# Hash-bucketed attention and a maxout FFN: heads 4 to 7 of the first batch as one set turned by VectorE, with new first copies, burst distance, halved sums and end buffers

## The chip, the core and the metric

The kernel runs on one core of a Trainium2 chip. The metric is the device time of one execution in microseconds (us); the time before is the median of three runs. A profile of one execution shows when each engine was busy: PE is TensorE's matmuls and PEld its weight loads, DVE is VectorE, ACT is ScalarE, POOL is GpSimd, and SP is SyncE, which here only issues transfers.

## The reference

Four batches of eight heads, 768 positions, head dimension 64. Each query and each key gets a bucket number from the signs of six projections; a query attends only to the keys of its own bucket. The attention output is the input of a feed-forward net with a maximum over three branches.

```python
q_bits = (np.einsum('bhsd,dk->bhsk', q, proj) > 0).astype(np.int64)
k_bits = (np.einsum('bhsd,dk->bhsk', k, proj) > 0).astype(np.int64)
q_bucket = np.sum(q_bits * powers, axis=-1)
k_bucket = np.sum(k_bits * powers, axis=-1)
mask = q_bucket[:, :, :, None] == k_bucket[:, :, None, :]
scores = np.where(mask, scale * np.matmul(q, k.transpose(0, 1, 3, 2)), -1000000000.0)
attn = softmax(scores)
x = np.matmul(attn, v) with the heads of one position side by side: (3072, 512)
h = np.maximum(np.maximum(x @ w1, x @ w2), x @ w3)
out = h @ w_out
```

Inputs and output are float32. The kernel rounds to bf16 and fp16 on the way; the hash projections are made in float32.

## The kernel before, in words

**Scores.** For each head the kernel builds a tile S of 72 rows: 64 rows of the transposed and scaled q (or k) and up to 8 rows of hash bits as plus or minus 0.5. One matmul of a k block with q columns gives the score and the number of equal bits at once, and the exponential (L301, ScalarE) is shifted so that keys of another bucket vanish. The work is cut into 192 units (`units`), each of 768 score columns: `scores(u)` makes two or three matmuls (L293) into a PSUM tile of which there are two, and one exponential into one of 24 weight tiles AT. Batch 0 is cut in three chunks of 256 queries (chunks 0 to 2, two units a head, 48 units in all), the others in two chunks of 384 (chunks 3 to 8, three units a head). Units 0 to 23 are heads 0 to 3 of batch 0, and units 24 to 47 heads 4 to 7; unit 24 is the first of head 4.

**Bursts.** When four heads of a chunk are done, a burst follows: `sums` adds the weights up by matmuls with ones (L345), VectorE makes reciprocals of them (L352 to L356), `values` multiplies the weights with v (L367, two sides), and VectorE writes the scaled result to xT (L374). From chunk 3 on, VectorE first adds the three AT tiles of a head into one of 768 columns (`add`, L324), and the sums run over its two halves. A burst of chunks 3 to 8 is placed two units after the last unit of its heads. In batch 0 the first three bursts stand at units 20 to 30, one piece to a unit.

**Feed-forward.** `ffn_groups(c)` gives groups of four matmuls (L396), whose maximum VectorE keeps (L405), and then the output rows (L433, copied by L437 and stored on SP's queue). A list `ffn` is worked off at about one group a unit; the rest runs behind the last unit. The output rows are copied to tiles `osb` of which there are two; the very last row block is made in two halves, copied by ScalarE (L418) and VectorE (L420).

**Where S comes from.** There are two ways.

- *Pairs* (heads 0 to 7 of batch 0, pairs 0 to 3): TensorE turns a head (`pair_turn`, L120, three transposes), VectorE or ScalarE copies it to T32 (`pair_keep`), GpSimd scales it into S (`pair_place`, L134), TensorE projects it (`pair_hash`, L147, or `head_hash`, L167), and VectorE writes the bits (L150 or L172); for pairs 2 and 3 the bits go to S by eight transfers on SP's queue (L156).
- *Sets of four heads* (all later ones): VectorE turns 32x32 blocks (`turn`, L198, four a side), GpSimd narrows to bf16 (`narrow`, L203, two a side), four transfers on SP's queue place the rows in S (`place`, L208), TensorE projects (`quad_hash`, L217), VectorE makes bits (L220), and four transfers on SP's queue send them to S (L228): k first half, k second half, q first half, q second half, each for all four heads.

**Order.** The order of instructions on each engine is the order in which the program writes them (a manual schedule). The loop over units writes the scores of unit u+1 and then what `when(u, ...)` has put there: loads, turns, copies; then feed-forward groups, and then the bursts. An engine, and each queue of transfers, works strictly in that order: a transfer written behind a waiting one on SP's queue waits with it, and so does an operation of GpSimd behind the loads that GpSimd issues. `load_v`, `load_weights` and most of `load_quad` are issued by GpSimd.

**The start.** Pair 0 is loaded in single heads. VectorE fills two columns behind each block of the AT tiles (L463). Meanwhile twelve matmuls on a tile called `warm` keep TensorE busy (L472). Then the first head is turned, copied, hashed and placed by hand-written steps, and unit 0 follows.

Of the kernel before, what the change touches and what calls it, by code (L numbers as in the profile page):

```python
# [17 lines left out]
def kernel(  # L18
# [15 lines left out]
    P = 128  # L34
# [19 lines left out]
    LAG = 1  # L54
# [25 lines left out]
    warm = at_tiles[-1][:, 0:HALF]  # L80
# [61 lines left out]
    def pair_hash(pi):  # L142
        i, bp = bank()
        for side in (1, 0):
            for hd in range(2):
                g = 2 * side + hd
                nc.tensor.matmul(bp[Q * g : Q * (g + 1), 0:HALF], pj2[:, :],  # L147
                                 t32[pi][:, side, hd * HALF : (hd + 1) * HALF], start=True, stop=True)
        bits = b_pool.tile([P, HALF], BF16, tag="bits", name="bits")
        nc.vector.tensor_scalar(out=bits[:], in0=bp[:, 0:HALF], scalar1=0.0, scalar2=0.5,  # L150
                                op0=AluOp.is_gt, op1=AluOp.subtract)
        give(i)
        for hd in range(2):
            for side in (1, 0):
                g = 2 * side + hd
                nc.sync.dma_start(s_of[pi][D : D + NBITS, g, :].rearrange("b (c n) -> b c n", c=2),  # L156
                                  bits[Q * g : Q * g + 2 * NBITS, :])


# [157 lines left out]
    def add(c, h, n):  # L317
# [67 lines left out]
    def ffn_groups(c):  # L385
# [23 lines left out]

        def last(part, tb):  # L410
# [5 lines left out]
            osb = o_pool.tile([P, DM], FP32, tag="osb", name="osb")  # L416
# [7 lines left out]
        for tb in range(w // P):  # L424
            def go2(part, tb=tb):
# [9 lines left out]
                if part == 1:  # L435
                    osb = o_pool.tile([P, DM], FP32, tag="osb", name="osb")
                    nc.scalar.copy(osb[:], ps[:, 0:DM])  # L437
                    give(k_)
                    nc.sync.dma_start(rows[block_of(b, q0 // P + tb)], osb[:])
# [8 lines left out]
    with tc.manual_schedule():  # L448
# [8 lines left out]
        load_pair(2, nc.sync)  # L457
        load_pair(3, nc.sync)
        nc.gpsimd.memset(pj[:], 0.0)
# [4 lines left out]
        for hd in range(2):  # L464
            for u in range(2):
                nc.vector.tensor_copy(pj2[hd * D + u * Q : hd * D + (u + 1) * Q, hd : hd + 2 * NBITS - 1 : 2], pst[:, u, :])
# [11 lines left out]
        i1, mk1 = bank()  # L478
        bq = sc_ps.tile([P, 2, 512], FP32, tag="sc", name="bp")[:, 0, :]
# [3 lines left out]
        pair_keep(0, 0, 0, mq)  # L483
        head_hash(bk, 0, 1, 0)
        head_hash(bq, 0, 0, 0)
        pair_turn(0, 1, 1, mk1)
        first_place(1, 0, 0, mk)
        head_bits(bk, 0, 1, 0, 0)
        first_place(0, 0, 0, mq)
        head_bits(bq, 0, 0, 0, 0)  # L490
        give(iq)
        first_place(1, 0, 1, mk)
        head_bits(bk, 0, 1, 0, 1)
        give(ik)
        give(ib)
        pair_place(0, 0, 1, 0, 1)
        i2, mq1 = bank()
        pair_turn(0, 0, 1, mq1)
        pair_keep(0, 1, 1, mk1, nc.scalar)
# [126 lines left out]
```

## Time and profile before

| | |
|---|---|
| median of 3 runs | 277.81 us (276.68 to 278.61) |
| the profiled execution | 277.43 us, its span 275.6 us |
| mean granted TensorE clock | 0.992 |
| exponentials (L301) | 192, 152.7 us, 816 ns each |
| feed-forward matmuls (L396) | 648, 115.0 us |
| score matmuls (L293) | 432, 93.5 us |
| value matmuls (L367) | 864, 37.7 us (four run at a time) |
| sums, chunks 3 to 8 (L345, 384 columns) | 96, 8.2 us |
| VectorE turns (L198) | 48, 26.6 us, 561 ns each |
| adds of weights (L324) | 96, 53.9 us |
| DMA moved | 30.97 MB, 114 GB/s over the span |

The span is the time from the first to the last instruction of the core; the execution's own time is a little longer. Busy times of different engines overlap. In lists of groups, each line names the line of the kernel, the engine, the operation, what is written and read, and how often; "idle before" is the engine's own idle time ahead of the instructions, with the one that ended it. In the timeline, a line is a run of equal instructions: start, length, engine, what, count, and in brackets the idle time before. SPq and POOLq lines are the issue of a transfer, not the transfer.

### The profile page before, as it was taken

What the parts mean: (1) busy time and instruction counts of PE and PEld (TensorE: products, weight loads), DVE (VectorE), ACT (ScalarE), POOL (GpSimd) and SP (SyncE); (2) the same over time, 40 slices, a digit from 0 to 9 for tenths busy, and PEclk for the clock granted to TensorE, in tenths of its full rate; (3) what the DMA queues carried; (4) which work ended last, traced back from release to release, by engine and by line L of the source; (5) the groups of instructions that cost most, each with busy time, mean ns of one, the idle gap of its engine ahead of it and who ended that gap; (6) DMA issues with size and microseconds to landing.
All of it is one profiled execution on the core that took longest, in us unless ns stands there. A gap on an engine that the chain in (4) does not pass through costs nothing.

```text
span 275.6 us, 6502 instructions
## 1 busy us (share of the span) xinstructions
PE 263.2 (95%) x2538; PEld 158.6 (58%) x2538; DVE 196.0 (71%) x486; ACT 179.1 (65%) x260; POOL 68.0 (25%) x108
## 2 busy tenths in 40 slices
PE   7899999999999979999999999999999999999992
PEld 3555667865666645565555555555555555555651
DVE  3686787965886996996684898797657674865440
ACT  2888876648767860966859586683868769571321
POOL 3699550374100350285000062140000000000000
PEclk9999999999999997999999999999999999999999
DMA  7979999979921157169912036622020003001203
GB/s 226 287 158 165 221 245 227 209 125 231 246 49 40 38 145 115 53 183 251 168 40 76 2 81 148 160 57 63 33 95 0 1 4 114 2 0 40 76 2 114
DMA packets 20398, 30.97 MB, mean 112 GB/s; under 512 B 2608, under 2 KB 14736, under 8 KB 20368
## 3 DMA queue, kind: packets, MB, share of 16 engines
q0 software_dynamic: 8384, 14.16, 26.9%
q1 hardware_dynamic: 11552, 15.88, 19.2%
q10 hardware_dynamic: 432, 0.52, 0.6%
q8 instruction: 20, 0.33, 0.5%
q14 instruction: 10, 0.08, 0.1%
HBM read 25.17 MB, written 6.29 MB: 114 GB/s over the span
## 4 chain that ended last, share of the span: by engine, by line
PE 86%; DVE 7%; ACT 2%; issue 2%; DMA 1%; DVEq 0%; ACTq 0%
PE ms L396 31%; PE sc L293 22%; PE ms L367 11%; PE ms L433 11%; PE ms L345 4%; PE ms L217 3%; ACT AT L301 2%; DVE ad L324 2%; PE ms L472 1%; DVE ht L405 1%; PE ms L120 1%; PE ms L147 1%; PE ms L167 1%; DVE S L172 1%; DMA out_dram<-osb 1%
## 5 line engine op out<-in xcount | busy, mean ns | idle before, releaser
L301 ACT ACTIVATE AT<-sc 128x768 f16<-128x768 f32 x192 | 152.7, 816 | 66.4 <-PE sc L293 58.6
L396 PE MATMUL ms<-xT,w_sb 128*128 128x384 f16 (+1 forms) x648 | 115.0, 308 | 0.7 <-DVE ht L405 0.7
L293 PE MATMUL sc<-S 72*128 72x384 bf16 (+1 forms) x432 | 93.5, 308 | 2.6 <-ACT AT L301 1.9
L396 PEld LDWEIGHTS <-w_sb 128*128 128x128 f16 x648 | 62.6, 97 | 36.9 <-issue 1.5
L405 DVE TENSOR_TENSOR ht<-ht,ms 128x384 f16<-128x384 f16 (+1 forms) x108 | 54.3, 503 | 37.3 <-PE ms L396 35.4
L293 PEld LDWEIGHTS <-S 72*128 72x128 bf16 (+1 forms) x432 | 39.5, 98 | 34.0 <-issue 14.1
L203 POOL TENSOR_SCALAR T<-T 128x768 bf16<-128x768 f32 x24 | 21.8, 907 | 101.2 <-DVE T L198 80.4
L367 PE MATMUL ms<-AT,vo 128*32 128x385 f16 (+3 forms) x864 | 37.7, 318 | 0.0
L433 PE MATMUL ms<-wout_sb,ht 128*128 128x512 f16 x138 | 35.4, 378 | 0.0
L367 PEld LDWEIGHTS <-vo 128*32 128x32 f16 x864 | 25.1, 99 | 9.3 <-issue 1.3
L324 DVE TENSOR_TENSOR ad<-AT,AT 128x768 f16<-128x768 f16 x48 | 27.4, 572 | 2.8 <-ACT AT L301 2.8
L324 DVE TENSOR_TENSOR ad<-ad,AT 128x768 f16<-128x768 f16 x48 | 26.5, 551 | 2.5 <-ACT AT L301 1.2
L198 DVE STREAM_TRANSPOSE T<-nat 128x384 f32<-128x384 f32 x48 | 26.6, 561 | 0.0
L401 ACT CAST ht<-ms 128x384 f16<-128x384 f32 x36 | 17.2, 477 | 8.8 <-PE ms L396 8.7
L374 DVE SCALAR_TENSOR_TENSOR xT<-ms,sv,rb 128x384 f16<-128x384 f32 (+1 forms) x36 | 19.9, 568 | 2.6 <-PE ms L367 1.3
L433 PEld LDWEIGHTS <-ht 128*128 128x128 f16 x138 | 13.3, 97 | 13.3 <-DVE ht L405 0.8
L437 ACT COPY osb<-ms 128x512 f32<-128x512 f32 x23 | 13.4, 582 | 10.7 <-PE ms L433 9.6
L352 DVE STREAM_TRANSPOSE ys<-ms 128x384 f32<-128x384 f32 (+1 forms) x18 | 9.7, 536 | 8.0 <-PE ms L345 7.8
L134 POOL TENSOR_SCALAR S<-T 64x384 bf16<-64x384 f32 (+1 forms) x21 | 13.2, 627 | 3.8 <-ACT T L127 1.6
L192 POOL DMA_DIRECT2D nat<-in_k_dram x20 | 11.1, 563 | 3.6 <-DMA nat<-in_k_dram 2.2
L192 POOL DMA_DIRECT2D nat<-in_q_dram x20 | 11.1, 566 | 2.7 <-DMA vo<-in_v_dram 1.8
L345 PEld LDWEIGHTS <-ones 128*32 128x32 f16 x240 | 5.4, 95 | 8.8 <-issue 8.7
(48 smaller groups left out, 121.9 us busy)
## 6 DMA issues: line engine op xcount, KB each, us to landing
out_dram<-osb SPq DMA_DIRECT2D x23, 256.0 KB
S<-T SPq DMA_DIRECT2D x48, 96.0 KB
nat<-in_k_dram POOLq DMA_DIRECT2D x20, 192.0 KB, 7.5
nat<-in_q_dram POOLq DMA_DIRECT2D x20, 192.0 KB, 7.1
vo<-in_v_dram POOLq DMA_DIRECT2D x8, 384.0 KB, 8.2
w_sb<-in_moe_w_dram POOLq DMA_DIRECT2D x3, 768.0 KB, 7.2
nat<-in_k_dram SPq DMA_DIRECT2D x6, 192.0 KB
nat<-in_k_dram SPq DMA_DIRECT2D x3, 384.0 KB
```

The costliest lines, as they stand in the source:

```text
L192: eng.dma_start(dst, src)
L198: nc.vector.transpose(t32[name][:, u, half * HALF : (half + 1) * HALF], i_)
L203: nc.gpsimd.tensor_scalar(out=t16[name][:, u, :], in0=t32[name][:, u, :], scalar1=RS, scalar2=1.0, op0=AluOp.mult, op1=AluOp.mult)
L293: nc.tensor.matmul(views[j], s_of[kn][0 : D + bits, kx, m * P : (m + 1) * P], s_of[qn][0 : D + bits, qx, q0 : q0 + w], start=True, stop=True)
L301: nc.scalar.activation(t[:, :, 0:w], whole, ActFn.Exp, bias=-SCALE * 0.25 * bits, scale=SCALE)
L324: nc.vector.tensor_tensor(out=sum_of[c, h][:], in0=t[0], in1=t[n], op=AluOp.add)
L367: nc.tensor.matmul(av[Q * x : Q * (x + 1), 0:n], v_at[2 * b + i][:, x, cb * D + side : (cb + 1) * D : 2], weights_of(c, 4 * i + x, m)[:, 0 ...
L374: nc.vector.scalar_tensor_tensor(out=xt_of(c)[:, 2 * i + side, 0:w], in0=av[:, 0:w], scalar=sv_of[b, i, side][:], in1=rb[0][:, 0:w], op0=A ...
L396: nc.tensor.matmul(ps[:, 0:w], w_sb[wi][:, jc, fb * P : (fb + 1) * P], xt[:, jc, 0:w], start=(jc == 0), stop=(jc == NJC - 1))
L401: nc.scalar.copy(hts[fb][:, 0:w], ps[:, 0:w])
L405: nc.vector.tensor_tensor(out=hts[fb][:, 0:w], in0=hts[fb][:, 0:w], in1=ps[:, 0:w], op=AluOp.max)
L433: nc.tensor.matmul(ps[:, 0:DM], hts[fb][:, tb * P : (tb + 1) * P], wout_sb[:, fb, :], start=(fb == 0), stop=(fb == NFB - 1))
```

## The change

- Heads 4 to 7 of batch 0 are no longer pairs 2 and 3 but set 1: two times four loads on SP's queue, VectorE's turns at units 6 to 9 (k) and 10, 12, 13, 14 (q), GpSimd's narrows at 7, 9, 12 and 14, the places at 9 and 14, the hash behind unit 16 and its bits at 17. The turned blocks of a set of batch 0 keep the key order that `block_of` expects.
- The start: `warm` uses 256 columns that no fill touches, in 14 matmuls; the first k copy is VectorE's and the first q copy ScalarE's; the first k rows are placed by GpSimd; the hash is made in single matmuls for each half, alternately for k and q; the copies of head 1 go from ScalarE to VectorE. Unit 0's scores stand before the transposes of head 1.
- On GpSimd, the clearing and filling of `pj` moves behind the start, `load_v(0)` to unit 2 and the k load of set 2 from unit 1 to unit 4. The operand pj2 is filled half by VectorE and half by GpSimd.
- Bursts of chunks 3 to 8 stand four units behind, not two; the hashes of sets 4 to 7 stand two units later.
- From chunk 4 on, VectorE adds the two halves of a head's summed weights once more, and the sums take one block instead of two.
- The output rows of the last chunk are copied into three parts of one large tile, not into the two `osb` tiles.

```diff
-    LAG = 1
+    LAG = (1, 4)
...
-    warm = at_tiles[-1][:, 0:HALF]
+    warm = at_tiles[-1][:, THIRD + 2 : 2 * THIRD + 2]
...
-    def head_hash(bp, pi, side, hd):
-        for par in range(2):
+    def head_hash(bp, pi, side, hd, pars=(0, 1)):
+        for par in pars:
...
-        i_ = nat[name].rearrange("p (cc m u d) -> p u m cc d", cc=CC, u=2, d=Q)[:, u, half * MH : (half + 1) * MH]
+        ms = slice(half, NM, 2) if name[1] == 1 else slice(half * MH, (half + 1) * MH)
+        i_ = nat[name].rearrange("p (cc m u d) -> p u m cc d", cc=CC, u=2, d=Q)[:, u, ms]
...
+        if n == 2 and c > 3:
+            t = sum_of[c, h]
+            nc.vector.tensor_tensor(out=t[:, 0, :], in0=t[:, 0, :], in1=t[:, 1, :], op=AluOp.add)
...
-            return [t[:, j, 0:w] for j in range(2)]
+            return [t[:, j, 0:w] for j in range(1 if c > 3 else 2)]
...
+        def out_rows(tb):
+            if c < NCH - 1:
+                return o_pool.tile([P, DM], FP32, tag="osb", name="osb")
+            if "end" not in nat:
+                nat["end"] = nat_pool.tile([P, 4 * NM * D], FP32, tag="nat", name="nat")
+            return nat["end"][:, tb * DM : (tb + 1) * DM]
...
-            osb = o_pool.tile([P, DM], FP32, tag="osb", name="osb")
+            osb = out_rows(tb)
...
-        load_pair(2, nc.sync)
-        load_pair(3, nc.sync)
-        nc.gpsimd.memset(pj[:], 0.0)
+        for side in (1, 0):
+            load_quad(side, 1, range(4), nc.sync)
...
-        for x in range(4):
-            nc.gpsimd.tensor_copy(pj[x * Q : (x + 1) * Q, :, x : x + 4 * NBITS - 3 : 4], pst[:])
-        load_v(0)
...
-        for n in range(12):
-            nc.tensor.matmul(wp[:, 0:HALF], warm[:, 0:P], warm, start=True, stop=True)
+        for n in range(14):
+            nc.tensor.matmul(wp[:, 0:THIRD], warm[:, 0:P], warm, start=True, stop=True)
...
         pair_keep(0, 1, 0, mk)
-        pair_keep(0, 0, 0, mq)
...
+        pair_keep(0, 0, 0, mq, nc.scalar)
+        give(ik)
+        for par in range(2):
+            pair_place(0, 1, par, 0, 1)
+        first_place(0, 0, 0, mq)
+        give(iq)
+        pair_place(0, 0, 1, 0, 1)
+        for par in range(2):
+            head_hash(bk, 0, 1, 0, (par,))
+            head_hash(bq, 0, 0, 0, (par,))
+        head_bits(bk, 0, 1, 0, 0)
+        head_bits(bq, 0, 0, 0, 0)
+        scores(0)
+        i1, mk1 = bank()
         pair_turn(0, 1, 1, mk1)
...
         pair_turn(0, 0, 1, mq1)
-        pair_keep(0, 1, 1, mk1, nc.scalar)
...
-        pair_keep(0, 0, 1, mq1, nc.scalar)
+        head_bits(bk, 0, 1, 0, 1)
+        head_bits(bq, 0, 0, 0, 1)
+        give(ib)
+        give(jb)
+        pair_keep(0, 1, 1, mk1)
+        give(i1)
+        pair_keep(0, 0, 1, mq1)
...
+        nc.gpsimd.memset(pj[:], 0.0)
+        for x in range(4):
+            nc.gpsimd.tensor_copy(pj[x * Q : (x + 1) * Q, :, x : x + 4 * NBITS - 3 : 4], pst[:])
...
-        when(10, pair_hash, 2)
...
-        when(17, pair_hash, 3)
...
-        when(1, load_quad, 1, 2, range(4), nc.gpsimd)
+        when(2, load_v, 0)
+        when(4, load_quad, 1, 2, range(4), nc.gpsimd)
...
-        hash_at = {}
+        for side, us in ((1, (6, 7, 8, 9)), (0, (10, 12, 13, 14))):
+            for n, u in enumerate(us):
+                when(u, turn, (side, 1), n // 2, n % 2)
+                if n % 2:
+                    when(u, narrow, (side, 1), n // 2)
+            when(us[3], place, (side, 1), range(4))
+        hash_at = {16: 1}
...
-            hash_at[{2: 33, 3: 47}.get(g, need - 11)] = g
+            hash_at[{2: 33, 3: 47}.get(g, need - 9)] = g
...
-            d = done_at[c, i] + (LAG if c < 3 else 2)
+            d = done_at[c, i] + LAG[c > 2]
```

More of the change, by code (lines that the diff above doesn't have):

```diff
@@ L140, in pair_group @@
         give(i)
[L142 to L157, printed above, removed]
     def first_place(side, hd, par, mp):
@@ L435, in go2 @@
                 if part == 1:
-                    osb = o_pool.tile([P, DM], FP32, tag="osb", name="osb")
-                    nc.scalar.copy(osb[:], ps[:, 0:DM])
+                    osb = out_rows(tb)
+                    nc.scalar.copy(osb[:, 0:DM], ps[:, 0:DM])
                     give(k_)
-                    nc.sync.dma_start(rows[block_of(b, q0 // P + tb)], osb[:])
+                    nc.sync.dma_start(rows[block_of(b, q0 // P + tb)], osb[:, 0:DM])
             gs += [lambda go2=go2: go2(0), lambda go2=go2: go2(1)]
@@ L477 @@
         ib, bk = bank()
-        i1, mk1 = bank()
-        bq = sc_ps.tile([P, 2, 512], FP32, tag="sc", name="bp")[:, 0, :]
+        jb, bq = bank()
         pair_turn(0, 1, 0, mk)
@@ L507 @@
                 pair_place(0, side, par, 1, 2)
-        for pi, us in ((1, ((0, 1, 0), (0, 0, 0), (3, 1, 1), (4, 0, 1))), (2, ((6, 1, 0), (7, 1, 1), (8, 0, 0), (9, 0, 1))),
-                       (3, ((13, 1, 0), (14, 1, 1), (15, 0, 0), (16, 0, 1)))):
+        nc.gpsimd.memset(pj[:], 0.0)
+        for x in range(4):
+            nc.gpsimd.tensor_copy(pj[x * Q : (x + 1) * Q, :, x : x + 4 * NBITS - 3 : 4], pst[:])
+        for pi, us in ((1, ((0, 1, 0), (0, 0, 0), (3, 1, 1), (4, 0, 1))),):
             for u, side, hd in us:
@@ L515 @@
                         when(u, pair_place, pi, side, par, hd, hd + 1)
-                elif hd == 1:
-                    for par in range(2):
-                        when(u, pair_place, pi, side, par)
         when(2, head_rest, 0, 1)
@@ L521 @@
         when(5, head_rest, 1, 0)
-        when(10, pair_hash, 2)
-        when(11, t32.pop, 2)
         when(11, head_rest, 1, 1)
         when(12, t32.pop, 1)
-        when(17, pair_hash, 3)
-        when(18, t32.pop, 3)
-        when(1, load_quad, 1, 2, range(4), nc.gpsimd)
+        when(2, load_v, 0)
+        when(4, load_quad, 1, 2, range(4), nc.gpsimd)
         when(17, load_v, 1)
```

17 lines of the change are left out of this document (2 added, 15 removed).

## The prediction, made before the changed kernel ran

> **What bounds the kernel now.** I read the page first, then TensorE's order of time, then the other engines in the stretches where TensorE is not dense. From the page, busy time and the slices:
>
> ```profile
> PE 263.2 (95%) x2538; PEld 158.6 (58%) x2538; DVE 196.0 (71%) x486; ACT 179.1 (65%) x260; POOL 68.0 (25%) x108
> POOL 3699550374100350285000062140000000000000
> DMA  7979999979921157169912036622020003001203
> ```
>
> TensorE is 95% busy over the whole, but POOL and the DMA engines are full in the first ten slices (6.9 us each) and nearly idle after. The table by stage (columns: busy and count of PE, PEld, DVE, ACT, POOL; then granted clock, DMA share, GB/s):
>
> ```profile
> 9.00:28.30 19.30, 17.78 (x143) 10.67 (x145) 13.24 (x25) 16.49 (x24) 17.49 (x30) 1.00 0.90 184
> 28.30:42.00 13.70, 13.70 (x321) 9.48 (x324) 11.06 (x32) 10.31 (x14) 7.21 (x9) 1.00 1.12 234
> 98.00:105.00 7.00, 4.46 (x41) 2.90 (x44) 6.28 (x16) 3.23 (x4) 2.68 (x3) 0.93 0.53 108
> 105.00:112.00 7.00, 7.00 (x83) 4.53 (x75) 4.83 (x12) 2.10 (x3) 0.00 (x0) 0.82 0.52 100
> ```
>
> Up to 28.3 the exponentials set the pace, and POOL is 17.5 of 19.3 us busy. From 28.3 TensorE is dense: what delays it there is lost one for one. In 98 to 112 VectorE is late and the granted clock falls. From the timeline, ScalarE's gaps, TensorE at units 23 and 24, POOL's queue, and SyncE's:
>
> ```profile
> 20.61 0.81 ACT L301 ACTIVATE AT<-sc 128x768 f16<-128x768 f32 x1 [1.37 <-PE sc L293]
> 27.00 2.21 ACT L301 ACTIVATE AT<-sc 128x768 f16<-128x768 f32 x3 [0.80 <-PE sc L293]
> 31.49 0.83 PE L293 MATMUL sc<-S 70*128 70x256 bf16 x6
> 10.25 3.43 POOL L134 TENSOR_SCALAR S<-T 64x384 bf16<-64x384 f32 x6 [0.40 <-ACT T L127]
> 22.46 0.76 POOL L244 DMA_DIRECT2D w_sb<-in_moe_w_dram  x1
> 23.22 2.23 POOL L192 DMA_DIRECT2D nat<-in_q_dram  x4
> 48.44 0.82 POOL L203 TENSOR_SCALAR T<-T 128x768 bf16<-128x768 f32 x1 [6.90 <-DVE T L198]
> 47.79 3.03 SPq L228 DMA_DIRECT2D S<-bits  x4
> ```
>
> The reader is to see that POOL's work comes back to back in the first 30 us, so each piece put into its queue delays all behind it. The tail, from the chain of waits and the list of waits:
>
> ```profile
> 269.51 0.59 ACT osb L437
> 270.12 2.01 DMA out_dram<-osb
> 272.30 0.42 DVE osb L420
> DVE osb L420 <- DMA out_dram<-osb: 4.8, 1, 4.8
> ```
>
> The sum is made against the profiled execution, 277.43 us (span 275.6 and 1.83 around it), 0.38 below the median of 277.81.
>
> **Part 1, start.** The warm-up matmuls (12 in 3.77 us from 1.67, 0.31 each) waited for VectorE's fills of the weight tiles, since their operand held filled columns. The new operand has none: they start near 1.15, and 14 of 256 columns take 14 x 0.21 = 2.9, ending near 4.1. The first transposes, at 5.11 and with no wait shown on their loads, can move 0 to 0.95 earlier; 0.7 is taken. The q copy goes to ScalarE beside VectorE's k copy, but the hashes still run 0.82 and the two bits 0.56 and 0.55, so nothing more is won.
>
> A page of the Trainium skill, "TensorE: Matmul & The Clock Gate" ("Why this matters for your kernels" and "Part 4: PE-mode transpose"), speaks against the shorter warm-up: TensorE should be busy for 4 us for its full clock, and transposes do not count as busy. The trace agrees in that the warm-up ran at half pace (0.31 for 384 columns, where four of L396 take 0.65). By that rule the transposes, hashes and first scores (0.82, 0.82, 0.49) could take double, some 1.5 us more, and the sum below would be 282.0.
>
> **Part 2, units 1 to 20.** Out go eight groups of three transposes, eight copies of 0.55, two four-matmul hashes (1.84 and 1.25 us on TensorE) and eight POOL copies of 0.83; in come eight VectorE turns (0.56), one set hash (L217: 1.43 for 16 records), four POOL narrows (0.82 to 0.91) and eight S<-T transfers. VectorE is level, with slack (13.24 of 19.3). ScalarE's gaps of 1.37 and 0.80 stand behind the pair hashes; the 0.39 behind a head's hash stays in part. The set hash makes one gap of about 0.8. Gain 1.4 to 1.8.
>
> So TensorE would reach unit 24 (head 4, its first scores at 31.49) some 2.3 us earlier, near 29.2. **That is where the plan breaks.** Before, head 4's S came from POOL by 22.5 (17.81 + 4.70, not shown above). Now each S row of heads 4 to 7 waits for POOL's last narrow of q, and in POOL's program order that stands behind the q load of set 2 (unit 13) and the second weights (unit 12). POOL's dense run starts when head 1's k copy is made, after all four bits: 9.58 - 0.7 + 0.5 = 9.4. From there: 12 copies of 64x384 at 0.585 apart (six in 3.43, the last 0.505) 7.0; pj's fill and four copies, moved here, 1.1; load_v(0), moved here, 0.9; two weights issues at 0.8, 1.6; eight nat issues, 4.5; four narrows with 0.08 between at 0.9, 3.6. Sum 18.7: the last narrow ends near 28.1. SyncE then issues four q places at 0.60, and behind them in its queue the four bits at 0.72: k first half, k second, q first half. Unit 24 needs the third: issued at 28.1 + 2.4 + 1.4 = 31.9. Its landing is not in the trace. Bounds: 2.0 us (the out_dram transfer above, engines nearly idle) and 7.7 (the q loads issued at 23.2, median to landing, on POOL's queue). The k loads issued at 13.6 took 4.0 at a DMA share of 0.76; these transfers are small, but share the engines with the weights and set 2, as in the row with 1.12. I take 4.0: unit 24 starts near 35.9, which is 4.4 later than before (2.4 to 8.1), and the gains of parts 1 and 2 are swallowed whole. TensorE is in order: scores 25, the sums and values of the next bursts, and with them VectorE's xT, queue behind it.
>
> The page "DMA: Bandwidth & Descriptors" ("Anatomy of one DMA") gives a fixed price near 2.0 us to a transfer. By it the sum would be 2.0 lower, 278.6; no run here shows a landing on SyncE's queue under load.
>
> **Part 3, the clock.** An idle time of 29.2 to 35.9 costs more than itself. In 98 to 105 TensorE sat 2.5 us idle, no single wait over 1.45, and the granted clock fell to 0.93 and 0.82: 7 x 0.07 + 7 x 0.18 = 1.75 us lost. Here the idle is longer and TensorE dense after it: 1.75 to 2.5, taken 2.0.
>
> **Part 4, units 73 to 87.** Bursts of chunks 3 to 8 come two units later, so a burst no longer waits for an add just issued (1.4 at 103.96, and 0.4 for a bank). At most 1.9 and the clock's 1.75 are won. But VectorE is the one that is late (6.28 of 7): it gets four half adds, and a burst's chain of 3.07 (0.58, 0.17, 0.23, 0.58, 0.12, 0.62, 0.15, 0.62) now falls among the turns instead of two units ahead. By pieces from one burst to the next, VectorE has 17.2 us of work where it had 15.2, less 1.5 us of TensorE work that now lies ahead of the wait. Taken: 0 (from 3.6 gained to 1.75 lost).
>
> **Part 5, sums.** Adding the halves spares 40 of L345's matmuls: 8 take 0.33 until the values start (74.11 to 74.45), so 0.165 each for ten bursts, 1.65. The adds' waits of 0.12 to 0.37 in the later bursts go too (0.4); the last burst waits one half add longer (0.3). Gain 1.8. The 40 half adds cost VectorE about 0.35 each, by L324 (768 columns, 0.55) and L405 (256 and 384 of fp32, 0.41 and 0.55): 14 us in all, hidden beside TensorE where VectorE is 65 to 80% busy; if that cover is gone, they are the bound.
>
> **Part 6, tail.** The last rows have a buffer of their own, so L420 waits for its matmuls only (L414 ends at 270.73) and not for the transfer until 272.13: copy at 270.8 instead of 272.30, gain 1.5. L418's 0.84 goes within it.
>
> **Sum:** +4.4 + 2.0 + 0 - 1.8 - 1.5 = +3.1, so 277.43 + 3.1 = 280.5 us.
>
> **Rivals.**
> - *The set is ready in time (0.16).* If the third bits land before 29.2, all gains count: 0.7 + 1.6 + 1.8 + 1.5 = 5.6, 271.8. It needs the last narrow before 23.3 even at 2.0 to land, 4.8 earlier than POOL's sum. For it: POOL has 3.6 us less of copies. Against: that sum with the old order gives back the old rows.
> - *Late, but cheaply (0.20).* Landing 2.0 and no loss of clock: 2.4 - 3.3 = -0.9, 276.5; with some of part 4 won, 274.5.
> - *VectorE becomes the bound (0.07).* Half adds and chains among the turns cost 3 to 5 us over chunks 4 to 8, on top of a late set: 283.5 to 285.
> - *An edit doesn't act (0.02).* Were the last rows' slices still tied to one another, the 1.5 stays: 282.0. The last copy's only wait in program order is on TensorE, so hardly.
> - The forecast with its bounds, 277 to 284.5: 0.55.
>
> **How the numbers follow.** About 1% (2.8 us) is what a measurement here can tell from no change: below 275.0 is faster, above 280.6 slower. Faster: 0.16 and a fourth of the cheap case, 0.21. Slower: half of the forecast's weight, the cold start's share in it and the VectorE case, with the rest of the unknowns upward, 0.46. The rest 0.33. The forecast's own range is 277 to 284.5; with the cheap case it is 274.5 to 284.5, leaving out the set in time and the worst of VectorE.
>
> **What would show it.** In the changed profile: TensorE idle before L276 at unit 24 with a DMA of S as releaser, from about 29 to 36; the last POOL narrow of four near 28; a granted clock under 0.9 near 36; no wait of the sums on ad; L413 at once after its matmuls. Wrong it is if POOL's narrow ends by 24, or if TensorE runs through unit 24 without a gap: then 272.

## The result, and the profile after

| | median | lowest to highest | runs |
|---|---|---|---|
| before | 277.88 us | 276.68 to 278.61 | 4 |
| after | 295.63 us | 293.97 to 298.27 | 4 |

The ratio is 1.065, interval 1.056 to 1.074: the change makes the kernel 17.75 us slower. Ratios, here and below, are to the kernel before as timed in the same session, with their 95% interval; they leave out runs more than 1.5% above a kernel's fastest (one of the four of e14 and two of e3), while medians hold all runs. The profiled execution of after is the slowest of its four (298.27 us, span 296.5), 2.6 us above the median.

From the profile's page of after, busy time, the slices of TensorE and its granted clock (7.4 us a slice):

```profile
PE 263.1 (89%) x2476; PEld 154.4 (52%) x2476; DVE 212.0 (72%) x524; ACT 178.2 (60%) x257; POOL 66.6 (22%) x108
...
PE   7878129999999997789959999899999999998995
...
PEclk9999855999999999999998999999999999999999
```

TensorE is busy for 263 us as before, and VectorE 16 us more. The new time is in a hole of TensorE in slices 5 and 6, with the clock halved in slices 6 and 7, and in smaller ones in slices 16 to 18 and 21. The list of TensorE's waits and the chain of waits name what ended them:

```profile
PE sc L276 <- DMA S<-bits: 14.8, 2, 11.8
PE ms L382 <- DVE ht L391: 2.7, 5, 0.7
```

```profile
25.94 9.91 DMA S<-T
35.87 6.87 DMA S<-bits
...
146.45 7.93 DMA S<-bits
```

Two waits for the bits of S hold 14.8 us; none such was in the kernel before. The chain shows two transfers in a row at the first of them: a copy of rows of S, issued at 25.94, lands 9.91 us later, and the third of the four copies of bits, the one that unit 24 needs, is issued only then, at 35.87. SyncE's own waits agree:

```profile
SPq L211 <- DMA S<-T: 2.2, 2, 1.8
```

The timeline of after (start, duration, engine and line), for the start, POOL's last narrowing of q and SyncE's queue, TensorE at unit 24, the second wait, and the tail:

```profile
1.67 3.15 PE L462 MATMUL ms<-AT 128*128 128x256 f16 x14 [1.67 <-DVE AT L455]
4.61 1.48 PE L120 MATMUL ms<-iden,nat 128*128 128x128 f32 x6
9.24 0.49 PE L276 MATMUL sc<-S 70*128 70x256 bf16 x3 [1.35 <-DVE S L154]
...
28.64 0.83 POOL L186 TENSOR_SCALAR T<-T 128x768 bf16<-128x768 f32 x1
...
24.58 7.37 SPq L191 DMA_DIRECT2D S<-T  x8
32.05 5.48 SPq L211 DMA_DIRECT2D S<-bits  x4
...
42.83 1.44 PE L276 MATMUL sc<-S 70*128 70x256 bf16 x6 [11.85 <-DMA S<-bits]
...
154.51 0.80 PE L276 MATMUL sc<-S 72*128 72x384 bf16 x2 [2.97 <-DMA S<-bits]
...
293.11 0.42 DVE L413 COPY nat<-ms 128x256 f32<-128x256 f32 x1 [3.27 <-PE ms L407]
```

Unit 24 starts at 42.83 where it had started at 31.49, and the score matmuls there run at half pace. The last narrowing ends at 29.47, near the 28.1 of the prediction; the rest is what lies between it and unit 24. The last copy now follows its matmuls, as foreseen.

To see where time is lost on the way, the starts of the exponentials of two profiles can be set against each other, unit by unit (the difference to before, us; the last column is the difference of the spans). These rows are worked out from the traces:

```
kernel                       u0    u12   u22   u24   u30   u80   u96   u108  u116  u140  u191  span
after                        0.8  -0.8  -0.6  11.6  15.4  15.4  16.8  20.0  20.9  21.7  21.7  20.9
e11 (queue quiet)            0.7  -0.9  -0.7   4.6   8.3   9.4  10.7  13.7  13.3  14.2  14.2  13.3
e7  (lag alone)              0.4   0.4   0.4   0.4   0.4   0.2  -2.1  -2.1  -2.3  -2.3  -2.6  -2.6
e8  (lag, hash later)        0.2   0.2   0.2   0.2   0.2   0.1  -2.1   1.2   3.7   3.5   3.0   3.0
e6  (half additions alone)   0.0   0.0   0.0   0.0   0.0   0.0   3.3   4.8   5.1   6.5   7.5   8.2
e10 (half additions, lag)   -0.3  -0.3  -0.3  -0.3  -0.3  -0.4   0.7   0.6   0.2   1.3   1.8   2.5
```

After loses 12.2 us at unit 24, 3.8 in the six units behind it at half clock, 5.5 between units 80 and 116, and a little more later.

### The profile page after: what moved, and what is told of

Same layout as the page of the kernel before. It is cut to its first block, busy times and chain, and to the rows that moved or that the text cites. A ratio compares the mean times of both kernels' runs of the same rounds, so it can differ in the third digit from the quotient of the medians.

```text
span 296.5 us, 6413 instructions
## 1 busy us (share of the span) xinstructions
PE 263.1 (89%) x2476; PEld 154.4 (52%) x2476; DVE 212.0 (72%) x524; ACT 178.2 (60%) x257; POOL 66.6 (22%) x108
## 4 chain that ended last, share of the span: by engine, by line
PE 66%; DVE 12%; DMA 10%; POOL 5%; issue 3%; ACT 2%; SPq 1%; DVEq 0%; POOLq 0%; ACTq 0%
PE ms L382 24%; PE sc L276 16%; PE ms L353 10%; PE ms L426 9%; DMA S<-bits 5%; DMA S<-T 5%; PE ms L331 3%; DVE ad L307 3%; DVE ht L391 2%; PE ms L200 2%; POOL S L134 2%; DVE T L181 2%; ACT AT L284 2%; DVE ad L310 1%; POOL T L186 1%
## 5 line engine op out<-in xcount | busy, mean ns | idle before, releaser
L276 PE MATMUL sc<-S 72*128 72x384 bf16 (+1 forms) x432 | 96.0, 316 | 20.3 <-DMA S<-bits 14.8
L186 POOL TENSOR_SCALAR T<-T 128x768 bf16<-128x768 f32 x28 | 25.5, 912 | 123.4 <-DVE T L181 95.3
L353 PE MATMUL ms<-AT,vo 128*32 128x385 f16 (+3 forms) x864 | 36.6, 317 | 0.2
L181 DVE STREAM_TRANSPOSE T<-nat 128x384 f32<-128x384 f32 x56 | 30.6, 559 | 0.0
L353 PEld LDWEIGHTS <-vo 128*32 128x32 f16 x864 | 23.5, 98 | 12.2 <-issue 4.7
L307 DVE TENSOR_TENSOR ad<-ad,AT 128x768 f16<-128x768 f16 x48 | 26.4, 551 | 2.1 <-ACT AT L284 1.1
L307 DVE TENSOR_TENSOR ad<-AT,AT 128x768 f16<-128x768 f16 x48 | 26.7, 556 | 0.4 <-ACT AT L284 0.4
L338 DVE STREAM_TRANSPOSE ys<-ms 128x384 f32<-128x384 f32 (+1 forms) x18 | 9.6, 536 | 21.2 <-PE ms L331 18.4
L310 DVE TENSOR_TENSOR ad<-ad 128x384 f16<-128x384 f16 x40 | 18.4, 459 | 1.4
L430 ACT COPY osb<-ms 128x512 f32<-128x512 f32 x21 | 12.2, 582 | 10.9 <-PE ms L426 7.2
L389 DVE CAST ht<-ms 128x256 f16<-128x256 f32 x18 | 7.4, 413 | 6.2 <-PE ms L382 6.1
L174 POOL DMA_DIRECT2D nat<-in_q_dram x20 | 11.2, 562 | 2.2 <-DMA vo<-in_v_dram 1.4
## 6 DMA issues: line engine op xcount, KB each, us to landing
w_sb<-in_moe_w_dram POOLq DMA_DIRECT2D x3, 768.0 KB, 11.6
```

The lines of the kernel that those rows point to most:

```text
L174: eng.dma_start(dst, src)
L181: nc.vector.transpose(t32[name][:, u, half * HALF : (half + 1) * HALF], i_)
L186: nc.gpsimd.tensor_scalar(out=t16[name][:, u, :], in0=t32[name][:, u, :], scalar1=RS, scalar2=1.0, op0=AluOp.mult, op1=AluOp.mult)
L276: nc.tensor.matmul(views[j], s_of[kn][0 : D + bits, kx, m * P : (m + 1) * P], s_of[qn][0 : D + bits, qx, q0 : q0 + w], start=True, stop=True)
L310: nc.vector.tensor_tensor(out=t[:, 0, :], in0=t[:, 0, :], in1=t[:, 1, :], op=AluOp.add)
L353: nc.tensor.matmul(av[Q * x : Q * (x + 1), 0:n], v_at[2 * b + i][:, x, cb * D + side : (cb + 1) * D : 2], weights_of(c, 4 * i + x, m)[:, 0 ...
```

## The experiments

Theory and rivals of the first four: set 1 is late either because of what stands ahead of its narrowings in POOL's order, or because of the transfers themselves, or the loss lies elsewhere in the change.

**e1, the change without set 1** (the parts of batch 0's heads 4 to 7 as before, all else of the change kept).

```diff
-        for side in (1, 0):
-            load_quad(side, 1, range(4), nc.sync)
+        load_pair(2, nc.sync)
+        load_pair(3, nc.sync)
...
+        when(10, pair_hash, 2)
...
+        when(17, pair_hash, 3)
...
-        hash_at = {16: 1}
+        hash_at = {}
```

> The changed kernel with pairs 2 and 3 put back for heads 4 to 7, all else as changed. Theory A (the set's S lands late: 12 us of waiting at unit 24 and some 4 us of half clock behind it) expects about 295.6 - 16 = 279.6, no wait over 1 us at unit 24 and no clock drop before 60 us. Theory B (VectorE, loaded with half adds and with burst chains among its turns, costs most of the loss) expects 290 or more.

Measured: 290.39 us (287.68 to 290.92), ratio 1.045 [1.038, 1.051]. So more than half of the loss is there without the set, as theory B expected, though not from VectorE alone: its profile has no wait at unit 24, but three other ones:

```profile
PE sc L294 <- DMA S<-bits: 3.5, 1, 3.5
PE ms L371 <- DMA vo<-in_v_dram: 2.7, 1, 2.7
PE ms L400 <- DVE ht L409: 2.7, 5, 0.7
```

The values of heads 4 to 7 come late near unit 33 (GpSimd issues their load at 31.97 us, where it was 29.01 before, and it takes 12.1), a wait that after does not have; the bits of set 5 come late at unit 108, and VectorE is late at the feed-forward's maxima.

**e2, set 1 alone in the kernel before.**

```diff
-        load_pair(2, nc.sync)
-        load_pair(3, nc.sync)
+        for side in (1, 0):
+            load_quad(side, 1, range(4), nc.sync)
...
+        for side, us in ((1, (6, 7, 8, 9)), (0, (10, 12, 13, 14))):
...
+        hash_at = {16: 1}
```

> The kernel before with set 1 alone for heads 4 to 7 (its own turns, narrows, places, hash and bits), the start, the loads and all else as before. POOL's dense run lacks pj's fill and load_v here, so the last narrow of q should end near 26 (29.5 in the changed kernel). Theory A expects unit 24 near 39 and 285 to 291 us; theory B expects about 278 to 280, as no half add and no burst is moved.

Measured: 291.34 us (288.37 to 292.35), ratio 1.048 [1.041, 1.056]. Unit 24 starts at 44.51, later than the 39 expected. Here a good part is lost before the wait (unit 22 is already 8.4 us late), as the table by windows shows (busy of PE, PEld, DVE, ACT, POOL, then granted clock, DMA share, GB/s):

```profile
8.00:13.00 5.00, 3.20 (x20) 2.24 (x17) 2.27 (x5) 2.52 (x5) 3.26 (x7) 0.82 1.18 215
13.00:18.00 5.00, 5.00 (x25) 2.58 (x23) 2.22 (x4) 3.62 (x6) 4.08 (x9) 0.50 1.09 235
```

The clock is halved from 11 us on, where TensorE does 25 matmuls in five us; the kernel before does 44 in the same window at full clock. The change without the set loses 12.9 us and the set alone 13.9, together far more than 17.75: some of each is not lost in the whole change, and the parts had to be taken smaller.

**e3, POOL's order** (the second weights and the q load of set 2 moved behind the set's narrowings).

```diff
-        for n, u in ((0, 3), (1, 12), (2, 21), (3, 31)):
+        for n, u in ((0, 3), (1, 15), (2, 21), (3, 31)):
...
-        when(13, load_quad, 0, 2, range(4), nc.gpsimd)
+        when(16, load_quad, 0, 2, range(4), nc.gpsimd)
```

> The changed kernel with the second weights (unit 12) and the q load of set 2 (unit 13) put behind the last narrow of set 1, at units 15 and 16. The last narrow should end near 26.4 instead of 29.5. If POOL's order is what makes the set late (A1), unit 24 comes 3 us earlier, at 39.8, and the time is about 292.5. If the S transfers are slow because they share the DMA engines with the loads of GpSimd's queue (A2), they also meet less of them and unit 24 comes 5 us earlier or more.

Measured: 298.03 us (294.72 to 299.28), ratio 1.066 [1.058, 1.075]. The last narrowing ends at 26.4 in the place of 29.5, three us earlier, the bits are issued from 30.93 in the place of 32.05, and yet unit 24 starts at 43.20. POOL's order, the step that the prediction took for the place where the plan breaks, does not decide here.

**e4, all three weights behind unit 24.**

```diff
-        for n, u in ((0, 3), (1, 12), (2, 21), (3, 31)):
+        for n, u in ((0, 24), (1, 25), (2, 26), (3, 31)):
...
-        when(13, load_quad, 0, 2, range(4), nc.gpsimd)
+        when(15, load_quad, 0, 2, range(4), nc.gpsimd)
```

> The changed kernel with the three weights loads moved to units 24, 25 and 26 and the q load of set 2 to unit 15, so that while the S rows of set 1 are sent only v and the two halves of set 2 are on GpSimd's queue. A1 (order on POOL) expects the last narrow near 26 and unit 24 near 39. A2 (sharing of the DMA engines) expects the third bits to land 4 to 6 us after the last narrow, unit 24 near 31, no wait over 3 us there, and 280 to 284 us in all.

Measured: 293.44 us (292.50 to 294.58), ratio 1.057 [1.051, 1.064]. The last narrowing ends at 25.3, the bits are issued from 28.84, and unit 24 starts at 39.89: still eight us behind the last issue. That is nearer to A1's 39 than to A2's 31, but the loads of set 2 were still on the DMA engines, and e3 speaks against A1; neither is settled by this run.

**e5, the end buffers alone.**

```diff
+        def out_rows(tb):
+            if c < NCH - 1:
+                return o_pool.tile([P, DM], FP32, tag="osb", name="osb")
...
-            osb = o_pool.tile([P, DM], FP32, tag="osb", name="osb")
+            osb = out_rows(tb)
```

> The kernel before with one edit: the last chunk's output rows go to a buffer of their own and no longer wait for an earlier row's DMA. Theory T1 (the wait of 4.79 us at the last rows was real time of the path): the last copy follows the last matmul at once, about -1.5 us as the prediction has it, 276.0 us, ratio 0.994. Rival T2 (the last output DMA's own landing sets the end, so that the copy's wait is filled anyway): 277.5 us, ratio 1.000 within 0.2%.

Measured: 275.87 us (275.11 to 278.01), ratio 0.993 [0.991, 0.996]. A gain of 2.0 us. The timeline of e5 at the end:

```profile
271.40 0.42 DVE L427 COPY nat<-ms 128x256 f32<-128x256 f32 x1 [3.27 <-PE ms L421]
```

The same copy stood at 272.30 before, behind the transfer of an earlier row.

**e6, the half additions alone.**

```diff
+        if n == 2 and c > 3:
+            t = sum_of[c, h]
+            nc.vector.tensor_tensor(out=t[:, 0, :], in0=t[:, 0, :], in1=t[:, 1, :], op=AluOp.add)
...
-            return [t[:, j, 0:w] for j in range(2)]
+            return [t[:, j, 0:w] for j in range(1 if c > 3 else 2)]
```

> The kernel before with one edit: from chunk 4 on VectorE adds the two halves of a sum of weights, 40 more additions, and TensorE sums one block in the place of two. Theory T1 (TensorE bounds this part): -1.8 us as the prediction has it, 275.7 us, ratio 0.994. Rival T2 (VectorE is as close to the bound here: 40 additions at the 0.459 us each that the profile after shows are 18.4 us, most of them in stretches where VectorE is already over 90% busy): 1 to 4 us slower, 278.5 to 281.5 us, with TensorE waiting for VectorE at the sums' line.

Measured: 287.30 us (285.61 to 288.03), ratio 1.034 [1.030, 1.037]: 9.4 us slower, more than twice the most that the rival asked for. The waits of TensorE in e6:

```profile
PE ms L348 <- DVE ad L327: 7.1, 7, 1.8
...
PE ms L399 <- DVE ht L408: 1.8, 3, 0.7
```

The sums wait 7.1 us for additions, where the kernel before had 1.8, and the feed-forward waits for VectorE too.

**e7, the lag of four alone** (bursts of chunks 3 and later four units behind).

```diff
-    LAG = 1
+    LAG = (1, 4)
...
-            d = done_at[c, i] + (LAG if c < 3 else 2)
+            d = done_at[c, i] + LAG[c > 2]
```

> The kernel before with one edit: the bursts of chunks 3 and later run four units behind the unit that finishes them and not two. Theory T1 (bursts already had their inputs in time): within 0.5% of 277.5 us. Rival T2 (the later bursts pile up against the next pieces and VectorE's normalising of the heads comes later, which moves the feed-forward work towards the end): 1 to 3 us slower.

Measured: 275.08 us (274.81 to 275.16), ratio 0.990 [0.987, 0.993]: a gain of 2.8 us, outside both expectations. The windows of e7 that the prediction showed for the kernel before:

```profile
98.00:105.00 7.00, 5.76 (x49) 3.22 (x47) 6.79 (x18) 3.33 (x5) 3.26 (x4) 1.00 0.52 131
105.00:112.00 7.00, 7.00 (x90) 4.32 (x87) 6.69 (x16) 4.05 (x6) 0.97 (x1) 1.00 0.72 120
```

TensorE is busy 5.76 of 7 us where it was 4.46, and the clock stays at 1.00 where it was 0.93 and 0.82. The sums' wait for additions falls from 1.8 to 0.4 us.

**e8, e7 with the hash two units later.**

```diff
-            hash_at[{2: 33, 3: 47}.get(g, need - 11)] = g
+            hash_at[{2: 33, 3: 47}.get(g, need - 9)] = g
```

> The kernel of e7 with one more edit: the hash of the later sets two units later (9 units ahead of need in the place of 11). Theory T1 (the wait of 2.97 us at unit 108 in the profile after comes from this edit: in the kernel before the bits' issue was 9.5 us ahead of unit 108 and two units are some 3 us): TensorE waits 2 to 4 us for the bits of set 5 at unit 108, and with the half clock that follows the kernel is 2 to 5 us slower than e7. Rival T2 (the wait is there only because the kernel after runs late against the transfers that GpSimd issues): no wait over 0.5 us at unit 108, the same time as e7 within 0.5%.

Measured: 279.69 us (278.79 to 281.18), ratio 1.007 [1.004, 1.010], 4.6 us slower than e7. The timeline of e7, and then of e8, has the issue of set 5's bits, and in e8 unit 108:

```profile
121.46 2.94 SPq L228 DMA_DIRECT2D S<-bits  x4
```

```profile
125.76 2.94 SPq L228 DMA_DIRECT2D S<-bits  x4
...
135.67 0.80 PE L293 MATMUL sc<-S 72*128 72x384 bf16 x2 [3.02 <-DMA S<-bits]
```

```profile
135.00:142.00 7.00, 6.33 (x20) 2.93 (x21) 1.57 (x4) 2.42 (x4) 0.00 (x0) 0.52 0.01 3
```

Two units are 4.3 us here. The bits then reach S 9.9 us after the first issue, three us too late, and the next seven us go at a clock of 0.52 (the window above, of e8). The edit is a line of the change that the prediction did not cost at all.

**e9, the two that gain, together** (e5's and e7's diffs on the kernel before).

> The kernel before with the two edits that gained alone: the end buffers (e5) and the bursts of chunks 3 and later four units behind (e7). Theory T1 (they act at different places, the bursts at unit 64 to 108, the buffers behind the last matmul): their ratios multiply, 0.993 x 0.990 = 0.983, 273.1 us. Rival T2 (both gain from the same thing, the clock window at 104 us that fell to half in the kernel before and not in e7): no more than e7's 275.1 us.

Measured: 273.82 us (273.51 to 274.27), ratio 0.986 [0.983, 0.990], 3.8 us faster than before. A little less than the product; its profile has one wait of 1.0 us for the bits of set 5 at unit 108, so with TensorE earlier even eleven units ahead are just too few.

**e10, the half additions with the lag of four** (e6's and e7's diffs together).

> The kernel of e7 with the half additions of e6. Theory T1 (the half additions lose only because a burst two units behind asks TensorE for the sum before VectorE has added it, 7.1 us of waits at the sums' line in e6): with four units behind the waits go and TensorE's saved block is a gain, 1 to 2 us faster than e7, 273.5 us. Rival T2 (VectorE's 18.4 us of additions are too much for the stretches where it is near its bound): still 2 to 9 us slower than e7, 277 to 284 us, with waits for VectorE somewhere else.

Measured: 281.30 us (280.22 to 282.15), ratio 1.014 [1.010, 1.017], 6.2 us slower than e7. The longer lag takes the waits at the sums away (1.2 us left of 7.1), but not the loss. Two windows, of e7 and then of e10 (PE, PEld, DVE, ACT, POOL, clock, DMA share, GB/s):

```profile
95.00:110.00 15.00, 13.56 (x146) 8.53 (x144) 14.58 (x36) 8.51 (x11) 6.11 (x8) 1.00 0.60 124
...
150.00:200.00 50.00, 50.00 (x432) 26.81 (x430) 39.95 (x84) 34.93 (x53) 10.10 (x12) 1.00 0.33 82
```

```profile
95.00:110.00 15.00, 11.55 (x125) 6.84 (x123) 14.59 (x36) 7.11 (x9) 5.69 (x8) 1.00 0.58 120
...
150.00:200.00 50.00, 47.59 (x409) 25.51 (x408) 44.85 (x97) 32.68 (x50) 10.34 (x12) 1.00 0.29 72
```

From 95 to 110 us VectorE is full without the additions (14.58 of 15 us), and with them TensorE does 2.0 us less. From 150 to 200, with VectorE at 44.9 of 50 us, TensorE is idle 2.4 us of a stretch that it had filled. At 90% busy there is no cover left: TensorE waits for the maxima of the feed-forward, which stand behind the additions in VectorE's order.

**e11, GpSimd's queue emptied while set 1 is copied** (the change, with these loads moved).

```diff
-        when(4, load_quad, 1, 2, range(4), nc.gpsimd)
-        when(17, load_v, 1)
-        for n, u in ((0, 3), (1, 12), (2, 21), (3, 31)):
+        when(18, load_quad, 1, 2, range(4), nc.sync)
+        when(3, load_v, 1)
+        for n, u in ((0, 24), (1, 25), (2, 26), (3, 31)):
...
-        when(13, load_quad, 0, 2, range(4), nc.gpsimd)
+        when(19, load_quad, 0, 2, range(4), nc.sync)
```

> The kernel after with GpSimd's DMA queue kept empty while set 1 is copied into S: the values of heads 4 to 7 are loaded earlier (unit 3), w1, w2 and w3 behind unit 24, and the keys and queries of set 2 by SyncE behind set 1's bits. Theory T1 (S of set 1 is late because its small packets take turns on the 16 DMA engines with GpSimd's loads): the bits land within 4 us of their issue, and unit 24's scores start at 33 to 36 us in the place of 42.8, with under 3 us of waiting. Rival T2 (the copies take as long by themselves, 8 to 10 us from the issue of the bits to unit 24): unit 24 at 38 us or later, as in e4 (39.9). The whole time says less, because what is moved is needed later: 285 to 294 us.

Measured: 292.54 us (290.85 to 294.28), ratio 1.056 [1.050, 1.062]. Unit 24 starts at 35.80, seven us earlier than in after, with a wait of 4.9 us where under 3 was expected, and the last of the bits moves 7.0 us after the first issue, not 4: one load of weights was issued at 25.2 us all the same. The whole gains 3.1 us at the median and not seven (the two profiles are of the slowest execution of the one and the fastest of the other), and the two intervals overlap.

**e12, the change with the hash back at eleven units.**

```diff
-            hash_at[{2: 33, 3: 47}.get(g, need - 9)] = g
+            hash_at[{2: 33, 3: 47}.get(g, need - 11)] = g
```

> The kernel after with the hash of the later sets back at 11 units ahead of need. Theory T1 (the wait of 2.97 us at unit 108 and the half clock behind it come from that edit alone, as e8 against e7 has it, 4.6 us): no wait for the bits at unit 108, 291 to 292 us. Rival T2 (in the kernel after, set 5 is late anyway): within 1 us of 295.6 us.

Measured: 293.08 us (290.78 to 293.72), ratio 1.054 [1.049, 1.059]. The wait at unit 108 is gone (the exponentials' difference goes from 12.8 at unit 104 to 13.0 at unit 108, where after goes from 16.4 to 20.0). The median falls by 2.6 us, short of the 3.6 to 4.6 expected, and the interval overlaps that of after; the direction is as the first theory has it, the size is not settled by this run. In this profile the clock was halved from 19 to 36 us, ahead of unit 24, which after's was not.

**e13, the queue quieter still** (e11 with the weights at units 27, 28 and 29), a single run.

```diff
-        for n, u in ((0, 24), (1, 25), (2, 26), (3, 31)):
+        for n, u in ((0, 27), (1, 28), (2, 29), (3, 31)):
```

> The kernel of e11 with w1, w2 and w3 three units later still, behind set 2's last narrowings, because in e11 w1 was issued at 25.2 us all the same and GpSimd's queue held 41% of the engines between 24 and 36 us. Theory T1 (GpSimd's loads on the shared DMA engines are the whole of what is late beyond the prediction): unit 24 at 33 to 34 us, 2 us after the last of the four bits' copies is issued. Rival T2 (a chain of eight small copies, four copies of bits and a landing takes 10 us after the last narrowing by itself): unit 24 at 35 to 36 us as in e11 (35.8). The whole time is not what is asked, since the feed-forward weights now come late: 290 to 300 us.

Measured: 291.85 us. TensorE no longer waits at unit 24. It gets there at 36.16, late by itself: in this execution its clock was halved from 19 to 36 us. So the start of unit 24 does not tell the two theories apart. The transfers do. The view of the DMA engines has for each queue its packets, MB and share of the 16 engines; first after, from 32 to 39 us, then e13, from 28 to 32 us, the stretches in which the bits were issued:

```profile
q0 software_dynamic: 515, 1.14, 73.9%
q1 hardware_dynamic: 479, 0.58, 34.4%
```

```profile
q1 hardware_dynamic: 294, 0.26, 22.3%
```

q0 is the queue that GpSimd issues to, q1 SyncE's. In e13 q0 is empty. The bits are the only packets of 768 bytes in q1 then, so their passage can be read from the trace's records (us):

```
kernel   bits issued from   first bits packet   last bits packet   unit 24 starts
after    32.05              38.67               42.35              42.83
e3       30.93              37.74               42.49              43.20
e4       28.84              33.60               39.68              39.89
e11      27.88              32.38               34.88              35.80
e13      28.06              29.50               31.88              36.16 (no wait)
```

With the other queue empty the first packet moves 1.4 us after its issue and the last 3.8 us after the first issue, 0.8 behind the end of the last. With loads beside them (after) it is 6.6 and 10.3 us. So for the copies the first theory holds: they are late by GpSimd's loads on the shared engines, not by their own chain.

**e14, e11 without the half additions and with the hash back.**

```diff
-            return [t[:, j, 0:w] for j in range(1 if c > 3 else 2)]
+            return [t[:, j, 0:w] for j in range(2)]
...
-            hash_at[{2: 33, 3: 47}.get(g, need - 9)] = g
+            hash_at[{2: 33, 3: 47}.get(g, need - 11)] = g
```

> The kernel of e11 without the half additions and with the hash at 11 units ahead, so that of the change the start, set 1 by VectorE, the lag of four and the end buffers are left. Theory T1 (the three losses act one after the other: half additions 6.2 us as e10 against e7, the hash 2.5 to 4.6 us): 292.5 - 6.2 - 3 = 283.3 us, within 2 us. Rival T2 (TensorE has so much slack behind the late set 1 that they overlap): 287 us or more.

Measured: 281.71 us (279.95 to 285.96), ratio 1.010 [1.005, 1.015]: by the ratios 12.7 us less than e11. The two losses by themselves (e10 against e7 and e8 against e7) are 6.5 + 4.7 = 11.2 by the ratios. With intervals of over 1 us on either side the losses add up within the noise, and the second theory fails.

**e15, e9 with the hash at twelve units.**

```diff
-            hash_at[{2: 33, 3: 47}.get(g, need - 11)] = g
+            hash_at[{2: 33, 3: 47}.get(g, need - 12)] = g
```

> The kernel of e9 with the hash of the later sets one unit earlier (12 units ahead of need). Theory T1 (in e9's profile TensorE still waits 1.0 us for the bits of set 5 at unit 108): the wait goes, 0.5 to 1 us less than e9, 273.0 us. Rival T2 (that wait was of the profiled execution alone): within 0.3% of 273.8 us.

Measured: 273.68 us (272.83 to 273.99), ratio 0.983 [0.980, 0.986]. The wait of 1.0 us is gone from the profile. Against e9's 0.986 [0.983, 0.990] the two intervals touch, so whether it is faster than e9 stays open; both are faster than before and after.

## Why the prediction was wrong

In one line: it forecast 280.5 us (274.5 to 284.5), slower by 3.1, and the kernel is slower by some 18. It had the late set, the idle TensorE and the halved clock in their place, with the releaser that it named. It missed two other losses that together weigh as much, 11.2 us by the parts below: one it took for a gain, and one it did not list.

By the ratios (times 277.9 us; the whole is 1.065, 18.1 us), the change comes apart like this:

| part | from | predicted | measured |
|---|---|---|---|
| lag of four and end buffers | e9 | 0 - 1.5 | -3.8 |
| half additions | e10 less e7 | -1.8 | +6.5 |
| hash two units later | e8 less e7 | not costed | +4.7 |
| start and set 1, queue quiet | e14 less e9 | | +6.6 |
| rest: set 1 beside GpSimd's loads, and what does not add | after less all these | | +4.0 |
| (the last two rows: start and set 1 together) | | (4.4 + 2.0) | (+10.6) |
| sum | | +3.1 | +18.0 |

- **Part 5 is the step that failed most.** "14 us in all, hidden beside TensorE where VectorE is 65 to 80% busy; if that cover is gone, they are the bound." Most half additions take what was estimated (32 of 40 take 0.36 us), but eight take 0.86, and all 40 come to 18.4 us in the place of 14. The cover was read as an average over long stretches. Where the additions fall it was not there: VectorE was at 6.28 of 7 us before, a row that the prediction itself showed, and in e7 it is at 14.58 of 15. The rival "VectorE becomes the bound" had the mechanism, a chance of 0.07 and 3 to 5 us; measured are 6.2 to 9.4.
- **The hash.** The diff moves it from 11 to 9 units ahead of need. It is no part of the working, and it costs 4.7 us: three of waiting, the rest at the halved clock.
- **Part 2, from the narrowing to unit 24.** The last narrowing was put at 28.1 and ended at 29.47. The third copy of bits was put at 31.9, straight behind the others in SyncE's queue, and was issued at 35.87, when a copy of rows from 25.94 had landed; the sum has no such wait. From there to unit 24 it took 7.0 us, where 4.0 (2.0 to 7.7) was taken. Of the 6.9 us by which unit 24 came after the forecast's 35.9, 1.4 are the narrowing's, 2.6 the issue's and 3.0 the landing's. A load's landing on an idle or another queue was no measure of many small packets behind others. That the last narrowing sets the time was wrong as well: three us earlier (e3) gained nothing. The page "DMA: Bandwidth & Descriptors" of the Trainium skill ("Queues, rings and completion order") says that each DMA engine takes turns between the queues that have work, a packet at a time. The trace agrees in direction: 10.3 us with GpSimd's queue at 73.9% of the engines, 3.8 with it empty. The fixed 2.0 us of that page of the Trainium skill ("Anatomy of one DMA"), which it states for transfers that GpSimd issues and which the prediction weighed and left, would have been too short here: the bits' last packet came 4.8 us behind the end of the last issue in after, and 0.8 in e13.
- **The gains of units 1 to 20** came as worked out: from +0.8 at unit 0 to -0.8 at unit 12, 1.6 (predicted 1.4 to 1.8). They are lost at unit 24, as said. In e12, e13 and e14 they are lost sooner, at a clock halved from 19 us on: unit 22 is 2.3 to 3.1 us late there.
- **Part 1** failed. The warm-up was put at 1.15 us and starts at 1.67 as before: the trace still gives VectorE's fills (L455) as what ends its wait, though its columns hold none of them. Whether that goes by the tile or by the range that a fill spans was not tried. In after the transposes start 0.66 earlier than before but take 1.48 in the place of 0.82, and unit 0's scores start at 9.24, 0.8 later than before and not 0.7 earlier. Over the profiles, the new start reaches unit 0 at 8.32 (e1) to 9.24 us and the old one at 8.10 (e2) to 9.26 (e15); none is near the 7.76 of the forecast. The rule that was weighed against this part, from the page "TensorE: Matmul & The Clock Gate" of the Trainium skill ("Why this matters for your kernels"), asks for 4 us of busy TensorE for the full clock. No run here shows that the shorter warm-up costs the 1.5 us put to it: e1 has it and transposes of 0.97 us, e15 has the old one and transposes of 1.49.
- **Part 3, the clock**: 2.0 taken, 3.8 measured in after (11.6 at unit 24 to 15.4 at unit 30). It is 2.0 in e3, whose wait is as long (12.2 us), so the size was within the spread of these executions.
- **Part 4**: 0 taken, between 3.6 gained and 1.75 lost. The lag alone gains 2.8, near the good end: the clock's 1.75 and the wait on the additions. With the half additions beside it (e10) the gain is gone, which is the doubt that kept the term at 0.
- **Part 6**: -1.5 taken, -2.0 measured in e5. Right.

What stays open: the 6.6 us of the start and set 1 with the queue quiet are not split, nor are the remaining 4.0. The emptied queue recovers 2.6 of the latter by the ratios of e11 and after, with overlapping intervals.

## What to carry to other kernels

Cost every line of a diff, one-number moves of a deadline above all, and read an engine's slack in the stretch where the new work lands, not over the whole: 40 additions of 0.36 to 0.87 us cost 6.2 us, because VectorE had no time left where they fell. A small copy on the critical path that shares the DMA engines with bulk loads is as late as those loads make it (10.3 us and not 3.8), so keep the loads back; making its producer three us earlier, with the loads still beside it, gained nothing (e3). Take a bundle apart before judging it: two of its edits alone make a kernel of 273.8 us, which no other here beats clear of the noise.

## What was not expected of the hardware

- What TensorE's halved clock costs does not follow the length of the wait ahead of it. Over the six units behind unit 24 the delay grows by 3.8 us in after and 2.0 in e3, behind waits of 11.9 and 12.2, and by 3.7 in e11, behind a wait of 4.9.
- The clock can be halved with no long wait at all. In e2 it is, from 11 us on, and TensorE's longest wait between the warm-up and unit 24 is 1.1 us. The page "TensorE: Matmul & The Clock Gate" of the Trainium skill ("Why this matters for your kernels") names idle gaps above some 3 us as what brings it; here it went with a stretch of light work (3.20 of 5 us busy at a clock of 0.82, then 0.50); that the light work brought it was not tried by itself. Set 1 takes transposes and hashes off TensorE, and four of the eight profiles with it have such a fall (e2, and e12, e13 and e14 from 19 us on), none of the nine with the pairs. It does not come each time: from 13 to 18 us TensorE is busy 4.18 of 5 us in after, which keeps its clock until the wait at unit 24, and 3.97 in e12, e13 and e14, where it was 4.92 before.
- The 40 half additions of one shape take 0.357 to 0.868 us in the same execution. The same eight are long in every kernel that has them, and each of the eight runs beside a narrowing of GpSimd; none of the 32 short ones does. That the narrowing holds them up was not tried by moving one. Two lines of after:

```profile
110.12 0.97 POOL L186 TENSOR_SCALAR T<-T 128x768 bf16<-128x768 f32 x1 [23.51 <-DVE T L181]
110.44 0.86 DVE L310 TENSOR_TENSOR ad<-ad 128x384 f16<-128x384 f16 x1
```
